# One recurrence kernel: the first inverse is served first, and other early work queues behind it

## The chip, the cores and the metric

The kernel runs on one core of a Trainium2 chip. The metric is the device time of one execution in microseconds (us); of several runs the median is taken. The engines are PE (matrix multiply), DVE (vector), ACT (scalar), POOL (GpSimd) and SP (whose queue issues most transfers). Each engine takes its own instructions strictly in order; semaphores make it wait for others.

## The reference

A linear-attention recurrence over 4 x 8 heads, 768 tokens and head size 40, followed by a mixture of experts. Cut to what matters:

```
for t in range(768):                       # per batch and head
    y[t] = r[t] @ state
    Sa = state @ a[t]
    state = state * w[t] - outer(Sa, b[t]) + outer(v[t], k[t])
x = y as [3072, 320]
P = exp(x @ w_gate - max), then 8 rounds of row and column normalisation
out = sum over 8 experts of P[:, e] * (relu(x @ w1[e]) @ w2[e])
```

## The kernel before

The 768 tokens are cut into 12 chunks of 64. Heads go in pairs, four pairs to a batch element, so the work comes in 12 x 4 = 48 units (chunk c, batch element b), numbered 0 to 47 in the order of need (unit 4c + b). Three kinds of work make up the first 500 us:

- **A preparation** (`prep`, one per unit, also numbered 0 to 47). It loads the unit's input (`inp`, 451.5 KB, SP queue), forms running products of the decay on DVE (`q` L124, its reciprocal L128, `g` L134), scales keys and `a` by them (`kb` L147, `ab` L153 and L154: on DVE for the first six preparations except that most `kb` are on POOL, later all on POOL), multiplies them on PE (`ll` L159, and the transposes `kt` L167), and puts the results into one of 20 operand sets (`sx` by DVE L169 and ACT; `bb`, `cc`). It sends `lt`, a part of the product, to DRAM (`ld`). POOL clears each set's `bb` once (L102).
- **An inverse** for each group of two chunks (`GROUPS`; 8 preparations, 128 small triangular matrices at once, one per partition). `load_lu` reads `ld` back into `lu` (L380), the steps of `INV` run on DVE (lines 184 to 207, nearly all through the scratch tile `pr`), `finish` (L369) flips the last part and writes the result to DRAM (`ud`, `nd`). `tload` reads it back in another layout for a chunk (`td`, `tt`, `lg`) and `tmat` completes it on PE and ACT (`gp` L261, `op` L266). An inverse needs the `ld` of all eight preparations of its group; a unit of chunks 0 and 1 needs inverse 0, of chunks 2 and 3 inverse 1, and so on up to inverse 5.
- **The recurrence** (`recur`, five steps for each unit): `av` on PE, `f` on DVE (L290), `xc` on PE, copies `x` and `c` on ACT, then `pu` on PE (L308), the first that needs the inverse, `pm` on DVE (L310), `c` on PE (L315), `ws` on DVE, `y` and `z` on POOL, and `zt` back to the next chunk's `vz`. I call the one `pu` of unit n "pu n"; it is 8 matmul records in the trace, 4 calls in the program.

Preparation n uses set n modulo 20, so preparations run up to 20 units ahead. From 500 us on, the experts run with PE nearly always busy.

The order on each engine is fixed when the kernel is built. `attention` makes a list `ev` of (time, function) with rule-of-thumb times, calls the functions in that order, and a scheduler then sorts each engine's instructions by that priority, the dependences, the free buffers and its own timing model. The first eight preparations have times from -20 on, the clears of `clear` come at `T_CLEAR`, the later preparations at -8 and above, and a step of chunk c at 5c and above; still, an instruction that could run early in the scheduler's model is placed early. Input tiles are borrowed from operand sets that are not yet in use (`IN_SETS`, `IN_SEQ`), as are the early `kb` and `lt` (`KB_SETS`).

## Time and profile before

| | |
|---|---|
| median of 3 runs | 1837.43 us (1831.14 to 1840.81) |
| profiled execution, its own time | 1831.31 us |
| its span in the trace | 1829.5 us |
| PE busy | 1729.6 us, 95% of the span |
| DVE / ACT / POOL busy | 1370.8 / 855.2 / 877.5 us |

"Busy" sums instructions of an engine; "granted clock" (PEclk) is the share of full TensorE speed in a stretch, so at 0.50 the same matmul lasts about twice as long and still counts as busy. Rows of the timeline give start, duration, engine, line, output<-input and a count. A row with SPq or ACTq is the issue of a transfer. Line numbers in rows of the profile are those of the kernel before.

### The profile page before, as it was taken

Reading aid. Unit: us, or ns where it says so; the run is one execution under the profiler, and the core shown is the slowest. Engines: PE = TensorE matmul, PEld = TensorE weight load, DVE = VectorE, ACT = ScalarE, POOL = GpSimd, SP = SyncE. Lnnn points to the kernel's source line nnn. Section 1 sums busy time; section 2 is a strip of 40 time slices with the busy share of each in tenths; the row PEclk is TensorE's granted clock in tenths of the full one; section 3 lists DMA queues with packets and bytes.
Section 4 is the critical chain, followed back from the end, with each engine's and each line's share of the span. In section 5 each row is a group of like instructions: output and inputs, shape, how many; then the busy total and the mean of one; then the engine's idle time right before and its main releaser. Section 6 shows DMA issues by size and latency. Waiting matters only on the chain.

```text
span 1829.5 us, 31656 instructions
## 1 busy us (share of the span) xinstructions
PE 1729.6 (95%) x11843; PEld 1701.8 (93%) x11843; DVE 1370.8 (75%) x2356; ACT 855.2 (47%) x1848; POOL 877.5 (48%) x851
## 2 busy tenths in 40 slices
PE   5479999999889999999999999999999999999999
PEld 4478889889879999999999999999999999999999
DVE  7876977974798867777686878977686877767676
ACT  6347767756643533434343434345343343424342
POOL 6545655721662626547191735007182644628160
PEclk8569999989899999999999999999999999999999
DMA  7467878766620101111020112201020111102001
GB/s 193 128 150 173 191 181 178 183 139 135 176 77 20 57 20 57 38 39 57 20 75 20 57 37 61 69 1 60 16 76 20 57 38 38 57 20 75 13 26 44
DMA packets 211759, 140.47 MB, mean 77 GB/s; under 512 B 162965, under 2 KB 193813, under 8 KB 211605
## 3 DMA queue, kind: packets, MB, share of 16 engines
q1 hardware_dynamic: 207925, 132.70, 27.9%
q10 hardware_dynamic: 3680, 5.74, 1.2%
q8 instruction: 94, 1.54, 0.4%
q14 instruction: 60, 0.49, 0.1%
HBM read 110.78 MB, written 27.61 MB: 76 GB/s over the span
## 4 chain that ended last, share of the span: by engine, by line
PE 77%; DVE 6%; DMA 4%; issue 4%; POOL 2%; SPq 2%; ACT 2%; ACTq 0%; POOLq 0%; DVEq 0%
PE op L647 36%; PE p L582 33%; PE xc L297 2%; DMA inp<-in_inp_dram 1%; PE ll L159 1%; PE pu L308 1%; PE c L315 1%; PE av L289 1%; DMA xs<-xd 1%; DVE g L134 1%; POOL ab L153 1%; PE op L266 1%; DVE hl L606 1%; DVE pr L193 1%; DVE q L124 1%
## 5 line engine op out<-in xcount | busy, mean ns | idle before, releaser
L582 PE MATMUL p<-xch,wh 128*128 128x384 f32 (+1 forms) x1792 | 605.3, 339 | 9.3 <-DVE sm L600 5.6
L603 ACT ACTIVATE hh<-sm 128x384 fp32r<-128x384 f32 x512 | 269.4, 526 | 725.4 <-DVE sm L600 725.4
L647 PE MATMUL op<-wh,hh 128*128 128x320 f32 x1536 | 476.5, 311 | 1.4 <-ACT hh L603 1.3
L647 PE MATMUL op<-wl,hh 128*128 128x320 f32 x1536 | 474.3, 309 | 0.0
L647 PE MATMUL op<-wh,hl 128*128 128x320 f32 x1536 | 466.7, 309 | 0.7 <-DVE hl L606 0.7
L528 POOL TENSOR_TENSOR wl<-ws,wh 128x640 fp32r<-128x640 f32 x60 | 103.1, 1718 | 606.1 <-ACT wh L526 605.8
L606 DVE SCALAR_TENSOR_TENSOR hl<-sm,hh 128x384 fp32r<-128x384 f32 x512 | 373.0, 762 | 2.3 <-ACT hh L603 2.0
L582 PEld LDWEIGHTS p<-xch,wh 128*128 128x128 f32 (+1 forms) x1792 | 337.4, 188 | 13.1 <-DVE sm L600 6.8
L582 PE MATMUL p<-xcl,wh 128*128 128x384 f32 x896 | 302.6, 338 | 0.0
L582 PE MATMUL p<-xch,wl 128*128 128x384 f32 x896 | 301.7, 337 | 0.0
L647 PEld LDWEIGHTS op<-wh,hh 128*128 128x128 f32 x1536 | 289.9, 189 | 2.2 <-ACT hh L603 2.2
L647 PEld LDWEIGHTS op<-wl,hh 128*128 128x128 f32 x1536 | 290.7, 189 | 0.0
L647 PEld LDWEIGHTS op<-wh,hl 128*128 128x128 f32 x1536 | 286.4, 188 | 1.1 <-DVE hl L606 0.9
L600 DVE TENSOR_TENSOR sm<-p,u 128x384 f32<-128x384 f32 x384 | 234.4, 620 | 8.8
L582 PEld LDWEIGHTS p<-xcl,wh 128*128 128x128 f32 x896 | 168.8, 188 | 0.0
L582 PEld LDWEIGHTS p<-xch,wl 128*128 128x128 f32 x896 | 168.6, 188 | 0.0
L600 DVE TENSOR_TENSOR sm<-p,p 128x384 f32<-128x384 f32 x128 | 71.3, 557 | 129.0 <-PE p L582 72.4
L600 DVE TENSOR_TENSOR p<-p,p 128x384 f32<-128x384 f32 x128 | 71.1, 556 | 101.2 <-PE p L582 100.6
L600 DVE TENSOR_TENSOR u<-p,p 128x384 f32<-128x384 f32 x128 | 70.7, 553 | 58.0 <-PE p L582 56.7
L536 POOL TENSOR_TENSOR wl<-ss,wh 128x512 fp32r<-128x512 f32 x60 | 89.8, 1497 | 30.8 <-ACT wh L533 26.7
L321 POOL TENSOR_TENSOR y<-ws,gl 104x256 f32<-104x256 f32 x48 | 43.1, 897 | 121.5 <-DVE ws L317 88.7
L159 PE MATMUL ll<-ab,kb 104*128 104x128 f32 x336 | 63.0, 345 | 37.2 <-POOL kb L147 16.7
(163 smaller groups left out, 2758.0 us busy)
## 6 DMA issues: line engine op xcount, KB each, us to landing
ws<-in_wts_dram SPq DMA_DIRECT2D x60, 832.0 KB, 4.5
inp<-in_inp_dram SPq DMA_DIRECT2D x42, 451.5 KB, 4.4
gd<-g SPq DMA_DIRECT2D x48, 113.8 KB, 2.8
gl<-gd SPq DMA_DIRECT2D x48, 113.8 KB, 2.9
vz<-in_v_dram SPq DMA_DIRECT2D x48, 112.0 KB, 3.3
xd<-y SPq DMA_DIRECT2D x24, 224.0 KB, 3.5
ld<-lt ACTq DMA_DIRECT2D x40, 128.0 KB, 2.7
rb<-in_r_dram SPq DMA_DIRECT2D x96, 48.0 KB, 2.9
```

The costliest lines, as they stand in the source:

```text
L124: nc.vector.tensor_tensor_scan(out=qr.rearrange("r p t -> r (p t)"), data0=w65[:, 260:0:-1], data1=one65, initial=0.0, op0=ALU.mult, op1=A ...
L134: nc.vector.tensor_tensor_scan(out=ge.rearrange("r p t -> r (p t)"), data0=w65[:, 0:260], data1=g1.rearrange("r p t -> r (p t)"), initial= ...
L159: nc.tensor.matmul(ll[:, p], lhsT=kb[:, p], rhs=ab[:, p], start=True, stop=True)
L297: nc.tensor.matmul(xc[h][:, p], lhsT=pp["sx"][:, p, h], rhs=f[:, p, h], start=True, stop=True)
L321: nc.gpsimd.tensor_tensor(out=y[0:R2, :, b % 2], in0=ws[:, :, 0:64], in1=gl[0:R2, :, 0:64], op=ALU.mult)
L528: g.tensor_tensor(out=wl[:, 0:640], in0=raw[:, 256:896], in1=wh[:, 0:640], op=ALU.subtract)
L536: g.tensor_tensor(out=lv[:, 3:7], in0=so[:, :, 0], in1=hv[:, 3:7, 0], op=ALU.subtract)
L582: nc.tensor.matmul(o, lhsT=w_, rhs=x_, start=(j == 0), stop=(j == 3))
L600: eng.tensor_tensor(out=out, in0=x, in1=y, op=ALU.add)
L603: nc.scalar.activation(out=hh[:, f, h], in_=sm[f][:, h], func=AF.Relu)
L606: v.scalar_tensor_tensor(out=hl[:, f, h], in0=sm[f][:, h], scalar=0.0, in1=hh[:, f, h], op0=ALU.max, op1=ALU.subtract)
L647: nc.tensor.matmul(ops[i], lhsT=a[:, h, cs], rhs=w_[:, cw], start=(f == 0 and h == 0 and j == 0), stop=(last and h == 1 and j == 2))
```

## The change

Nine inputs instead of six are borrowed or taken at the start (`IN_SETS` and `IN_SEQ` name more sets), and `g1`, `q`, `kb` and `lt` get two buffers instead of one. The first eight `ld` stores are issued by ACT instead of SP. Half of the second chunk's `load_lu`, the `nd` stores of inverse 0 and the four `tt` loads of chunk 0 go from SP to ACT as well, and chunk 0's `tload` is called inside `finish`. The memsets of `clear` are split: those that the first preparations need come at the very start, the rest (`lg`, `c1`, `tt`, `y`) go to POOL behind a mark. `mark` remembers one instruction of an engine, and `behind(...)` adds, for every instruction made inside it, an ordering edge to the mark of its own engine. The marks are: on ACT and SP the last `load_lu` transfers of inverse 0 (on ACT, for the clears, the last of the eight stores), on DVE the last copy of inverse 0, on POOL the last `ab` of preparation 7. Behind the marks go the steps of chunk 0 and preparations 9 to 19. Preparation 8 is left free. The scratch area reserved for software-made transfers is set to 1024 bytes; the kernel issues its transfers from SP and ACT.

```diff
-    g1_b = [pin.tile([RL, NP, 65], F32, name=f"g1{i}") for i in range(1)]
+    g1_b = [pin.tile([RL, NP, 65], F32, name=f"g1{i}") for i in range(2)]
...
+    for t in vz_b + rb_b:
+        nc.vector.memset(t, 0.0)
+    for t in (unf, tnf):
+        nc.gpsimd.memset(t, 0.0)
+    nc.gpsimd.memset(unf[:, 0:1024:33], 1.0)
+
     def clear():
-        nc.gpsimd.memset(unf, 0.0)
-        nc.gpsimd.memset(unf[:, 0:1024:33], 1.0)
-        nc.gpsimd.memset(tnf, 0.0)
-        for t in vz_b + rb_b + c1_b + lg_b:
-            nc.vector.memset(t, 0.0)
-        for t in y_b:
-            nc.gpsimd.memset(t[96:RL], 0.0)
-        for t in tt_b:
-            nc.gpsimd.memset(t, 0.0)
+        with behind(mybir.EngineType.Pool):
+            for t in lg_b + c1_b + tt_b:
+                nc.gpsimd.memset(t, 0.0)
+            for t in y_b:
+                nc.gpsimd.memset(t[96:RL], 0.0)
+
+    marks = {}
+
+    def mark(ins):
+        marks[ins.ins.engine] = ins.ins
+        return ins
+
+    def behind(*engines):
+        stack = ExitStack()
+        for e in engines:
+            stack.enter_context(tc.issue_after(marks[e]))
+        return stack
...
+    def send_l(c, b, lt, ld):
+        s, cc = GRP[c]
+        m = nc.scalar.dma_start(out=ld[cc, :, b], in_=lt)
+        if c * NB + b == N_FIRST - 1:
+            mark(m)
...
-        qr = pin.tile([RL, NP, 65], F32, name="q")
+        qr = pin.tile([RL, NP, 65], F32, name="q", bufs=2)
...
-            kb = pin.tile([R2, NP, 2, 64], F32, name="kb")
-            lt = pin.tile([64, NP, 2, 64], F32, name="lt")
+            kb = pin.tile([R2, NP, 2, 64], F32, name="kb", bufs=2)
+            lt = pin.tile([64, NP, 2, 64], F32, name="lt", bufs=2)
...
-        eng.tensor_tensor(out=ab[64:104, :, 64:128], in0=a_in[64:104], in1=g[64:104], op=ALU.mult)
+        m = eng.tensor_tensor(out=ab[64:104, :, 64:128], in0=a_in[64:104], in1=g[64:104], op=ALU.mult)
+        if cb == N_FIRST - 1:
+            mark(m)
...
-                nc.sync.dma_start(out=tt[r, :, r], in_=ud[u[blk][h]].rearrange("g j s -> j g s"))
+                (nc.sync if c else nc.scalar).dma_start(
+                    out=tt[r, :, r], in_=ud[u[blk][h]].rearrange("g j s -> j g s"))
...
-        nc.vector.tensor_copy(out=tn[us, 16:32, 0:16], in_=un[us, 0:16, 16:32].rearrange("u c j -> u j c"))
+        last = nc.vector.tensor_copy(out=tn[us, 16:32, 0:16], in_=un[us, 0:16, 16:32].rearrange("u c j -> u j c"))
         for o in range(0, us.stop, 64):
             nc.sync.dma_start(out=invs[s][1][o:o + 64], in_=un[o:o + 64])
-            nc.sync.dma_start(out=invs[s][2][o:o + 64], in_=tn[o:o + 64])
+            (nc.sync if s else nc.scalar).dma_start(out=invs[s][2][o:o + 64], in_=tn[o:o + 64])
+            if s == 0 and o == 0:
+                mark(last)
+                tload(0)
...
-                    nc.sync.dma_start(
+                    m = (nc.scalar if s == 0 and cc and h else nc.sync).dma_start(
...
+                    if s == 0 and cc and not h:
+                        mark(m)
...
-        next(gens[c, b], None)
+        with behind(*(() if c else marks)):
+            next(gens[c, b], None)
...
-        preps[c, b] = prep(c, b, invs[s][0])
+        with behind(*(marks if N_FIRST < c * NB + b < NSX else ())):
+            preps[c, b] = prep(c, b, invs[s][0])
...
-IN_SETS = (16, 15, 14, 13)
+IN_SETS = (16, 15, 14, 13, 18, 17, 19)
-IN_SEQ = (16,15,14,13,0,0,16,15)
+IN_SEQ = (16, 15, 14, 13, 18, 17, 0, 0, 19, 16, 15, 18, 17)
-N_SP = 8
+N_FIRST = 8
-T_CLEAR = -19.95
+T_CLEAR = -19.925
```

What this does to the order shows at three places. In the rows below the numbers behind names (`ab_203`) tell buffers apart; lines are those of each kernel's own file, and the changed file is 21 to 24 lines longer there (L124 becomes L145, L159 L182, L167 L190, L169 L192, L308 L332, L310 L334).

On DVE, the first steps of inverse 0. Before (`st` as the output is `sx` of a preparation):

```order
L200 COPY lu<-lu 128x2x8x8
L201 COPY lu<-lu 128x16x16
L184 TENSOR_TENSOR pr<-un,lu 128x4
L134 SCALAR_TENSOR_TENSOR g<-inp,g_205 112x260
L187 TENSOR_REDUCE un<-pr 128x4
L184 TENSOR_TENSOR pr<-un,lu 128x16
L187 TENSOR_REDUCE un<-pr 128x4x2
L169 TENSOR_TENSOR st_158<-ll,cst 64x8x64
L184 TENSOR_TENSOR pr<-un,lu 128x36
```

The same place now, from the last two `sx` of the first eight preparations on:

```order
L192 TENSOR_TENSOR sx_187<-ll,cst 64x8x64
L192 TENSOR_TENSOR sx_190<-ll,cst 64x8x64
L223 COPY lu<-lu 128x2x8x8
L224 COPY lu<-lu 128x16x16
L207 TENSOR_TENSOR pr<-un,lu 128x4
L210 TENSOR_REDUCE un<-pr 128x4
L207 TENSOR_TENSOR pr<-un,lu 128x16
L210 TENSOR_REDUCE un<-pr 128x4x2
```

Between the first and the last row of inverse 0, DVE had 26 instructions of other preparations; now it has one, the `sx` of preparation 8.

On DVE, where inverse 1 begins. Before, between the last copy of inverse 0 (L369) and the start of inverse 1 (L200) stand the four instructions of one preparation:

```order
L369 COPY tn<-un 128x16x16
L124 SCALAR_TENSOR_TENSOR q<-inp,cst 112x260
L128 RECIPROCAL g_205<-q 112x4
L134 SCALAR_TENSOR_TENSOR g<-inp,g_205 112x260
L169 TENSOR_TENSOR st_165<-ll,cst 64x8x64
L200 COPY lu<-lu 128x2x8x8
L201 COPY lu<-lu 128x16x16
```

Now 53 instructions stand there (11 `q`, 11 reciprocals, 11 `g`, 8 `sx`, 5 `f`, 3 `ws`, 4 `pm`); the last of them and the start of inverse 1:

```order
L341 TENSOR_TENSOR ws<-c_1332,c_206 104x416
L334 TENSOR_TENSOR pm<-pu,cst 128x416
L145 SCALAR_TENSOR_TENSOR q<-inp,cst 112x260
L149 RECIPROCAL g_200<-q 112x4
L155 SCALAR_TENSOR_TENSOR g<-inp,g_200 112x260
L223 COPY lu<-lu 128x2x8x8
L224 COPY lu<-lu 128x16x16
```

So inverse 1 went from before the first `pm` to behind the fourth. From its first row to its last copy DVE now has the 39 instructions of the inverse, 2 copies of inverse 2's input, 10 `sx`, 9 `q`, 8 reciprocals, 7 `g`, 5 `f`, 5 `ws`, 4 `pm` and 2 small copies `lg`; inverse 2 begins in the row after it.

On PE, the rows ahead of the first `pu`. Before:

```order
L159 MATMUL ll<-ab_204,kb 128x128 x4
L167 MATMUL kt<-cst,kb 128x104 x4
L261 MATMUL gp<-td,lg 64x32 x8
L266 MATMUL op<-td,lg 64x32 x8
L261 MATMUL gp<-td,lg 64x32 x8
L308 MATMUL pu<-x_948,tt_199 128x104 x4
```

Now:

```order
L285 MATMUL gp<-td,lg 64x32 x8
L182 MATMUL ll<-ab_197,kb 128x128 x4
L190 MATMUL kt<-cst,kb 128x104 x4
L290 MATMUL op<-td,lg 64x32 x8
L285 MATMUL gp<-td,lg 64x32 x6
L182 MATMUL ll<-ab_198,kb 128x128 x4
L190 MATMUL kt<-cst,kb 128x104 x4
L285 MATMUL gp<-td,lg 64x32 x2
L332 MATMUL pu<-x_939,tt_193 128x104 x4
```

Preparations now stand between the steps that complete the inverse, but there are fewer of them ahead of the first `pu`. Counted over the PE order, and over the DVE order for the inverses:

| ahead of pu number | 1st | 4th | 8th | 9th | 14th | 24th | 48th |
|---|---|---|---|---|---|---|---|
| preparations begun, before | 18 | 20 | 24 | 24 | 31 | 40 | 48 |
| preparations begun, now | 12 | 17 | 24 | 29 | 32 | 41 | 48 |
| matmul calls, before | 184 | 284 | 452 | 490 | 708 | 1124 | 1996 |
| matmul calls, now | 136 | 260 | 444 | 528 | 720 | 1128 | 2002 |

| last copy of inverse | 0 | 1 | 2 | 3 | 4 | 5 |
|---|---|---|---|---|---|---|
| stands behind pm number, before | none | 4 | 13 | 22 | 30 | 36 |
| now | none | 8 | 12 | 20 | 28 | 37 |

Inverse 1 is needed from the 9th `pu` on, inverse 2 from the 17th, inverse 3 from the 25th, inverse 4 from the 33rd, inverse 5 from the 41st.

More of the change, by code (lines that the diff above doesn't have):

```diff
@@ L161, in prep @@
             nc.scalar.activation(out=lt, in_=ll[64:128], func=AF.Copy, scale=-1.0)
-            (nc.sync if cb < N_SP else nc.scalar).dma_start(out=ld[GRP[c][1], :, b], in_=lt)
+            send_l(c, b, lt, ld)
             kt = pt.tile([128, NP, 2, 64], F32, name="kt", tag="pt")
@@ L177, in prep @@
         if cb >= NKB:
-            (nc.sync if cb < N_SP else nc.scalar).dma_start(out=ld[GRP[c][1], :, b], in_=lt)
+            send_l(c, b, lt, ld)
         return dict(cc=cc, g=gd, sx=sx, bb=bb)
@@ L400, in attention @@
         t = 5 * c + 2 - T_LEAD
-        ev.append((t - L_LEAD, tload, (c,)))
+        if c:
+            ev.append((t - L_LEAD, tload, (c,)))
         for half in range(2):
@@ L823 @@
     from concourse.bass_utils import run_bass_kernel_spmd as _run
-    nc = _bacc.Bacc("TRN2", target_bir_lowering=False, num_devices=1)
+    nc = _bacc.Bacc("TRN2", target_bir_lowering=False, num_devices=1, dynamic_dma_scratch_size=1024)
     lay = _layout(inputs)
```

## The prediction

> **What bounds the kernel now.** I read the top of the page first, then a table of stretches, then the timeline around the inverses, and the DVE and POOL groups of the early stretches.
>
> ```profile
> span 1829.5 us, 31656 instructions
> PE 1729.6 (95%) x11843; PEld 1701.8 (93%) x11843; DVE 1370.8 (75%) x2356; ACT 855.2 (47%) x1848; POOL 877.5 (48%) x851
> 4.00:8.00 4.00, 0.00 (x0) 0.00 (x0) 3.64 (x7) 3.63 (x11) 3.88 (x5) 1.00 1.01 295
> 56.00:76.00 20.00, 8.82 (x39) 7.54 (x38) 18.54 (x41) 7.13 (x19) 11.22 (x13) 0.50 0.43 126
> 76.00:96.00 20.00, 8.32 (x36) 7.35 (x36) 19.14 (x23) 7.93 (x21) 13.14 (x13) 0.50 0.46 120
> 136.00:156.00 20.00, 19.80 (x206) 18.80 (x205) 17.49 (x29) 16.35 (x42) 17.07 (x20) 1.00 0.83 199
> 172.00:227.00 55.00, 49.73 (x463) 47.16 (x462) 51.34 (x90) 38.89 (x98) 35.18 (x41) 0.94 0.84 188
> 600.00:1829.00 1229.00, 1223.75 (x7691) 1222.59 (x7689) 907.57 (x1542) 495.20 (x976) 568.78 (x490) 1.00 0.13 43
> ```
>
> The stretches give, after their length, the busy time of PE, weight loads, DVE, ACT and POOL, then the granted clock, the DMA share and GB/s. From 600 us on PE is busy 1223.75 of 1229 us: nothing there can move, and a gain or loss of the first 500 us arrives whole at the end. From 56 to 96 us, inverse 0, DVE is full (37.7 of 40) and PE is half empty at half clock. From 136 us on PE is nearly full; from 172 to 227, inverse 2, DVE is again the fuller (51.3 of 55 against 49.7). So three things can be bought: an earlier first `pu`, fewer stretches in which an inverse fills DVE, and less waiting for an inverse.
>
> **The change, part by part.** The stations of the run before:
>
> ```profile
> 7.37 0.63 DVE L124 TENSOR_TENSOR_SCAN q<-st,cst 112x260 f32<-112x260 f32 x1
> 23.55 0.70 DVE L124 TENSOR_TENSOR_SCAN q<-st,cst 112x260 f32<-112x260 f32 x1
> 37.71 0.66 DVE L124 TENSOR_TENSOR_SCAN q<-st,cst 112x260 f32<-112x260 f32 x1
> 46.61 0.68 DVE L169 TENSOR_TENSOR sx<-ll,cst 64x512 f32<-64x512 f32 x1 [0.49 <-PE ll L159]
> 56.32 0.27 DVE L200 COPY lu<-lu 128x128 f32<-128x128 f32 x1 [0.61 <-DMA ld<-lt]
> 97.53 0.57 DVE L369 COPY tn<-un 128x256 f32<-128x256 f32 x1
> 113.67 2.03 PE L308 MATMUL pu<-x,tt 128*128 128x104 f32 x8
> 148.34 0.37 DVE L369 COPY tn<-un 128x256 f32<-128x256 f32 x1
> 177.38 1.14 PE L308 MATMUL pu<-x,tt 128*128 128x104 f32 x8
> 226.00 1.04 PE L308 MATMUL pu<-x,tt 128*128 128x104 f32 x8
> 308.71 1.84 PE L308 MATMUL pu<-x,tt 128*128 128x104 f32 x8
> 377.56 1.06 PE L308 MATMUL pu<-x,tt 128*128 128x104 f32 x8
> 393.35 1.43 PE L308 MATMUL pu<-x,tt 128*128 128x104 f32 x8
> ```
>
> The `q` rows are preparations 0, 3 and 7, the `sx` is preparation 7's; inverse 0 runs from 56.32 to 98.1, inverse 1 ends at 148.7; the `pu` rows are the 1st, 9th, 14th, 24th, 32nd and 33rd.
>
> Step 1, inverse 0 starts earlier. From preparation 0 to 3 the pace was 16.2 / 3 = 5.4 us each, from 3 to 7 14.2 / 4 = 3.5, because the first three share DVE, POOL and SP with the clears and with chunk 0's first `av`, `f` and `xc`. These now stand behind inverse 0, so all eight go at 3.5: the last `q` at 7.4 + 7 x 3.54 = 32.2 instead of 37.7. From the last `q` to the inverse it was 18.6 us. On POOL, clears of later sets stood ahead of the last `kb`, on SP inputs and `gd` of later preparations ahead of the stores; without these I take 14, so the inverse starts at 46. Bounds: 11 us from the last `q` (43), or all 18.6 (51). The nine inputs are 4.06 MB; at the 295 GB/s of 4 to 8 us they take 14 us and are in by 18, ahead of their use at 32, so this early load costs nothing; the cover goes if the preparations run faster than 2 us each.
>
> Step 2, inverse 0 alone on DVE. Its 34 instructions through `pr`, and the means of the others that DVE runs there:
>
> ```profile
> 105.00:149.00 44.00, 24.02 (x34) 0.78 0.72 148
> L124 DVE TENSOR_TENSOR_SCAN q<-inp,cst 112x260 f32<-112x260 f32 x5 | 3.9, 783 | 1.4 <-DMA inp<-in_inp_dram 1.4
> L134 DVE TENSOR_TENSOR_SCAN g<-inp,g 112x260 f32<-112x260 f32 x4 | 2.8, 688 | 0.0
> L290 DVE TENSOR_TENSOR f<-av,cst 104x512 f32<-104x512 f32 x4 | 2.7, 669 | 1.4 <-PE av L289 1.4
> L169 DVE TENSOR_TENSOR sx<-ll,cst 64x512 f32<-64x512 f32 x4 | 2.7, 667 | 0.0
> L317 DVE TENSOR_TENSOR ws<-c,c 104x416 f32<-104x416 f32 x4 | 2.3, 571 | 0.0
> L310 DVE TENSOR_TENSOR pm<-pu,cst 128x416 f32<-128x416 f32 x4 | 2.3, 563 | 0.0
> L128 DVE RECIPROCAL g<-q 112x4 f32<-112x4 f32 x5 | 0.8, 165 | 0.0
> ```
>
> 24.0, five copies of at most 0.37 and one `sx` (0.67) are 26.4 us, where it took 41.8. Preparation 8's `sx` is late on POOL (it stands behind some 6 us of clears), but POOL starts on these while the stores land, so I cost that wait at nothing, at most 3 us. Inverse 0 ends at 46 + 26.4 = 72.4, 25.7 us earlier than at 98.1.
>
> Step 3, to the first `pu`: it was 15.6 us. Two `nd` stores and four `tt` loads leave SP, but preparations 9 to 11 now begin only at 72.4 and stand on PE ahead of this `pu`. POOL makes them:
>
> ```profile
> L147 POOL TENSOR_TENSOR kb<-inp,q 104x512 f32<-104x512 f32 x11 | 14.0, 1270 | 17.2 <-DVE q L124 11.3 <-PE kt L167 3.5 <-issue 1.1
> L154 POOL TENSOR_TENSOR ab<-inp,g 40x256 f32<-40x256 f32 x10 | 9.1, 914 | 0.8
> L153 POOL TENSOR_TENSOR ab<-inp,g 40x256 f32<-40x256 f32 x10 | 8.9, 888 | 8.7 <-issue 6.6 <-DVE g L134 2.2
> L152 POOL COPY st<-q 104x4 f32<-104x4 f32 x8 | 4.0, 498 | 7.2 <-DVE q L124 7.1
> L102 POOL MEMSET st<- 128x416 f32 x6 | 2.5, 443 | 0.7 <-DMA ld<-st 0.6
> ```
>
> That is 3.6 us for each preparation, 4.0 with the clear: 12 us for three, then their `ll` and `kt`. So I leave 15.6: the first `pu` at 88.0 (85 to 92), a lead of 25.7.
>
> Two pages bear on this step. The transfers first: four `tt` issues on SP took 2.08 us.
>
> ```profile
> 105.35 2.08 SPq L252 DMA_DIRECT2D tt<-ud  x4
> 106.00:116.00 10.00, 7.55 (x60) 7.19 (x60) 7.86 (x23) 3.77 (x10) 1.39 (x2) 0.50 0.96 191
> 126.00:136.00 10.00, 10.00 (x89) 9.55 (x89) 8.64 (x12) 5.82 (x14) 5.87 (x5) 0.91 0.45 111
> ```
>
> The Trainium skill ("Trainium Kernel Development and Optimization", Key Constraints) says that SP and ACT issue to the same 16 DMA engines, so that a second issuing engine saves only issue time; the DMA share of 0.96 above agrees that the engines themselves are taken. By it the moved issues save at most those 2.08 us here, and the sum would end at 1824 instead of 1826.
>
> The clock second: PE idles through inverse 0, so the work behind it starts at half clock, as from 56 to 96 us. From 106 to 116 PE was busy 7.55 of 10 us and still had 0.50; 0.91 came with 126 to 136. The Trainium skill ("TensorE: Matmul & The Clock Gate", Part 1) gives full rate after one busy window of about 3.4 us, which would save some 4 us of PE work ahead of the first `pu` and end at 1822 at best; the stretch above does not bear it out, so half clock until well behind the first `pu` is in my sum.
>
> Step 4, inverse 1 is pushed back. It used to run from 106 to 148.7 beside chunk 0. Now 53 DVE instructions lie between inverse 0 and 1: 11 `q` 8.6, 11 reciprocals 1.8, 11 `g` 7.6, 8 `sx` 5.3, 5 `f` 3.3, 3 `ws` 1.7, 4 `pm` 2.3, together 30.6 us. But POOL has nine preparations (9 to 17) there, 9 x 3.57 = 32.1, six clears 2.7, and by estimate 5 for three pairs of `y` and `z` (1.6 a pair, less than a `kb` and an `ab`, since their tiles are smaller): 40 us. POOL is later than DVE, so inverse 1 starts at 72.4 + 0.7 + 40 = 113. Behind it DVE has 25.7 of the inverse, 0.6 of copies, 10 `sx` 6.7, 9 `q` 7.0, 8 reciprocals 1.3, 7 `g` 4.8, 5 `f` 3.3, 5 `ws` 2.9, 4 `pm` 2.3, `lg` 0.3: 54.9. In 105 to 149 such a sum was used up without a hole, so inverse 1 ends at 168 (DVE alone: 158; with as much waiting again as POOL adds: 178). The 9th `pu` comes 15.6 later, at 183.6, where it was 177.4. The lead of 25.7 is a lag of 6.2. Who waits: all of chunk 2, and PE, which from the 8th `pu` on has only preparations left.
>
> Step 5, what is bought with it. The five preparations that PE has more behind it at the 9th `pu` are work of the next stretch, and inverse 2, which began at 172.5 and filled DVE until 227, now follows inverse 1 at once. From the 9th to the 14th `pu` it took 48.6 us for 218 calls, 0.223 each; from the 14th to the 24th 82.7 us for 416 calls, 0.199, where PE sets the pace. Now there are 192 calls, and with inverse 2 largely done I take the pace of PE: 38.2 us, the 14th `pu` at 221.8 instead of 226.0, a lead of 4.2 us. One preparation is still ahead there: its `ll` and `kt` are 1.68 us.
>
> ```profile
> 181.29 1.16 PE L159 MATMUL ll<-ab,kb 104*128 104x128 f32 x8
> 190.74 0.52 PE L167 MATMUL kt<-cst,kb 104*128 104x104 f32 x4
> 171.53 5.03 DMA inp<-in_inp_dram
> ```
>
> Step 6, less waiting for inverses 3 and 4. They ended two units ahead of their use, now four. The 33rd `pu` came 15.8 us after the 32nd, where a unit takes 8.3; so up to 7.5 us were lost there. I take 5 (0 to 12, since inverse 3 may give some as well). The larger buffers and the smaller scratch area cost nothing by themselves.
>
> Sum: -4.2 - 1.7 - 5 = -10.9 us. The profiled execution took 1831.3 us (span 1829.5 and 1.8 around it), which gives 1820.4. It lies 6.1 below the median of the runs shown, 1837.4; against that median, 1826.
>
> **The rivals.**
>
> (a) Much better, 1814. POOL is not late: alone, `kb` and `ab` are shorter than these means, which come from a stretch where DVE was full. Then inverse 1 starts with the 30.6 of DVE, 9.4 us earlier, and two later waits go: -11 - 9.4 - 3 = -23. For it: the means are high against the shortest rows. Against it: DVE is just as full now.
>
> (b) No change, 1835 to 1838. Step 5 pays nothing, because PE is at 49.7 of 55 there anyway: then the lag of 6.2 stands against five preparations of 1.68 (8.4), -2 us, and step 6 may be another issue order and give nothing. The same comes out if the change does not do what it says: if the first eight preparations keep 5 us each, inverse 0 starts at 54, all is 8 us later, and -11 becomes -3.
>
> (c) Slower, 1846. SP is in order too. Behind the inverse it gets `load_lu` of inverse 1 ahead of the inputs of preparations 16 on, and the first four of those loads wait for the store of preparation 11. An input took 5.03 us on the chain (row above); if four of them (16 to 19) are fetched one after the other, 20 us are added to step 4, inverse 1 ends at 188 and the 9th `pu` at 204. -11 + 20 = +9. It decides once inverse 1 ends later than 188; the prefetch of six inputs ahead of the inverse speaks against it.
>
> **How the numbers follow.** My case gets 0.42, (a) 0.18, (b) 0.28, (c) 0.12. Half a per cent, 9.2 us, is about what a measurement of this kernel can tell from no change; that is 1828.2. Of my case (1818 to 1834 by the bounds of steps 1, 4 and 6) some two thirds lie below, 0.28, which with (a) makes 0.46 faster; 0.14 and (b) make 0.42 the same; (c) is 0.12 slower. The range is 1811 to 1843: it cuts (c) at its lower half and the far end of (a).
>
> **What would show it.** Right: the first `lu` copy near 46, the last copy of inverse 0 near 72, the first `pu` near 88, inverse 1 from about 113 to 168, the 9th `pu` near 184 and the 14th near 222; POOL full from 73 to 113. Wrong: a first `lu` copy behind 51 (step 1), a hole of several us in inverse 0 at preparation 8's `sx` (step 2), a DVE that waits for inputs between the inverses (rival c), or a 9th to 14th `pu` no closer than before (step 5).

## The result: slower, and inverse 1 is 21 us later than forecast

The changed kernel took 1854.53 us (median of 5 runs, 1849.85 to 1860.02), beside 1837.43 for the kernel before (5 runs, 1831.14 to 1841.80). The ratio is 1.0096, with a 95% interval of 1.0069 to 1.0124: 17 us slower, where 1826 was forecast. The profiled execution took 1851.92 us, so it stands 2.6 below its median, as that of before stood 6.1 below; spans of single profiles are therefore compared with some caution, and the verdicts below rest on medians.

The top of the page, and then the stretches that answer to those of the prediction (length; busy time of PE, weight loads, DVE, ACT, POOL; granted clock, DMA share, GB/s):

```profile
span 1850.1 us, 31613 instructions
PE 1734.0 (94%) x11843; PEld 1705.3 (92%) x11843; DVE 1360.1 (74%) x2354; ACT 855.6 (46%) x1848; POOL 869.3 (47%) x854
49.00:76.00 27.00, 4.31 (x20) 3.65 (x19) 25.56 (x40) 1.86 (x5) 1.27 (x3) 0.50 0.61 145
80.00:100.00 20.00, 18.80 (x114) 17.57 (x113) 10.02 (x17) 14.36 (x36) 14.71 (x24) 0.50 0.64 129
100.00:120.00 20.00, 19.86 (x181) 18.98 (x180) 8.66 (x15) 14.29 (x35) 10.05 (x15) 0.91 0.89 168
180.00:200.00 20.00, 6.12 (x28) 5.27 (x28) 15.03 (x29) 8.85 (x25) 10.11 (x12) 0.55 0.84 191
```

The engines do the same work as before (PE 1734.0 us against 1729.6), so the loss is mostly waiting. The first stretch is inverse 0: DVE is full, and PE, ACT and POOL together do 7.4 us of work in 27. Between 80 and 120 it is the other way round: PE has hardly a free us and DVE is busy 18.7 of 40. From 180 to 200 PE has 6.1 us of work in 20, because units from the 9th on wait for inverse 1.

The stations, as rows of the timeline (start, duration, engine, line, operation, in brackets the idle time ahead of it and what ended it):

```profile
49.30 0.27 DVE L223 COPY lu<-lu 128x128 f32<-128x128 f32 x1 [7.98 <-DMA lu<-ld]
75.90 0.37 DVE L393 COPY tn<-un 128x256 f32<-128x256 f32 x1
97.29 2.03 PE L332 MATMUL pu<-x,tt 128*128 128x104 f32 x8
134.09 0.27 DVE L223 COPY lu<-lu 128x128 f32<-128x128 f32 x1 [0.89 <-DMA rb<-in_r_dram]
191.99 0.35 DVE L393 COPY tn<-un 128x256 f32<-128x256 f32 x1
208.13 2.01 PE L332 MATMUL pu<-x,tt 128*128 128x104 f32 x8
250.30 0.39 PE L332 MATMUL pu<-x,tt 128*128 128x104 f32 x2
520.00 1.03 PE L332 MATMUL pu<-x,tt 128*128 128x104 f32 x8
```

Inverse 0 runs from 49.3 to 76.3 and ends 22 us earlier than before. But inverse 1 starts at 134.1 (before 106.3), ends at 192.3 (148.7), and the 9th `pu` comes at 208.1 (177.4), the 14th at 250.3 (226.0; the row has its first two records), the 48th at 520.0 (498.65). The lead of 22 us is a lag of 31 at the 9th `pu`, and 21 of it reach the end.

What DVE waited for from 76 to 135, and POOL and ACT from 50 to 135 (sum, times, longest):

```profile
DVE q L145 <- DMA inp<-in_inp_dram: 16.0, 5, 4.9
DVE q L145 <- POOL kb L168: 3.9, 2, 2.0
POOL kb L168 <- DVE q L145: 26.8, 1, 26.8
ACT st L178 <- DMA td<-ud: 29.1, 1, 29.1
```

POOL and ACT stand still for 27 and 29 us, the whole of inverse 0: nothing is left for them that is not queued behind it. (The text on the change names the last `load_lu` as ACT's mark for the preparations too; in the code only SP's `load_lu` is marked, and ACT's mark is the last of the eight stores. So it is through `q` on DVE, and through ACT's own `nd` and `tt` transfers, that the two stand still.) And the five `q` that wait for inputs, those of preparations 15 to 19, stand on DVE ahead of inverse 1, such as these two:

```profile
104.86 0.78 DVE L145 TENSOR_TENSOR_SCAN q<-inp,cst 112x260 f32<-112x260 f32 x1 [4.90 <-DMA inp<-in_inp_dram]
131.55 0.70 DVE L145 TENSOR_TENSOR_SCAN q<-inp,cst 112x260 f32<-112x260 f32 x1 [3.82 <-DMA inp<-in_inp_dram]
```

### The profile page after: what moved, and what is told of

Its sections match the earlier page's. It is cut to its first block, busy times and chain, and to the rows that moved or that the text cites. A ratio compares the mean times of both kernels' runs of the same rounds, so it can differ in the third digit from the quotient of the medians.

```text
span 1850.1 us, 31613 instructions
## 1 busy us (share of the span) xinstructions
PE 1734.0 (94%) x11843; PEld 1705.3 (92%) x11843; DVE 1360.1 (74%) x2354; ACT 855.6 (46%) x1848; POOL 869.3 (47%) x854
## 4 chain that ended last, share of the span: by engine, by line
PE 73%; DVE 4%; DMA 1%; issue 1%; ACT 1%; POOL 0%; SPq 0%; ACTq 0%; DVEq 0%; POOLq 0%
PE op L679 35%; PE p L614 32%; PE xc L321 1%; DVE hl L638 1%; PE pu L332 1%; PE av L313 1%; DVE sm L632 1%; PE c L339 1%; PE op L290 1%; PE gp L285 0%; PE lp L369 0%; PE zt L359 0%; DVE u L632 0%; DMA inp<-in_inp_dram 0%; DVE p L632 0%
## 5 line engine op out<-in xcount | busy, mean ns | idle before, releaser
L632 DVE TENSOR_TENSOR sm<-p,p 128x384 f32<-128x384 f32 x128 | 71.3, 557 | 130.3 <-PE p L614 72.7
L632 DVE TENSOR_TENSOR u<-p,p 128x384 f32<-128x384 f32 x128 | 70.8, 553 | 58.9 <-PE p L614 57.8
L743 DVE SCALAR_TENSOR_TENSOR acc<-op,pmat,acc 128x320 f32<-128x320 f32 x168 | 91.3, 544 | 4.5 <-PE op L679 4.4
## 6 DMA issues: line engine op xcount, KB each, us to landing
ld<-lt ACTq DMA_DIRECT2D x42, 128.0 KB, 3.0
```

The costliest lines, as they stand in the source:

```text
L632: eng.tensor_tensor(out=out, in0=x, in1=y, op=ALU.add)
L743: nc.vector.scalar_tensor_tensor(out=acc[:, m], in0=ops[i], scalar=pmat[:, n, e:e + 1], in1=acc[:, m], op0=ALU.mult, op1=ALU.add)
```

## The experiments

All are edits of the changed kernel. The stations of each, from its trace (us; the time between the end of inverse 0 and the start of inverse 1 stands in the fourth column), and its median:

| run | inverse 0 | inverse 1 starts | behind inverse 0 | 9th `pu` | 48th `pu` | median | ratio to before, 95% |
|---|---|---|---|---|---|---|---|
| before | 56.3 to 98.1 | 106.3 | 8.2 | 177.4 | 498.7 | 1837.4 | 1 |
| changed | 49.3 to 76.3 | 134.1 | 57.8 | 208.1 | 520.0 | 1854.5 | 1.0069 to 1.0124 |
| e1 four inputs | 45.8 to 73.3 | 125.7 | 52.4 | 201.4 | 512.7 | 1843.2 | 1.0012 to 1.0052 |
| e2 16 to 19 held on DVE | 47.9 to 74.8 | 124.9 | 50.0 | 201.8 | 518.5 | 1850.7 | 1.0040 to 1.0104 |
| e3 `gd` on ACT | 47.8 to 74.7 | 130.7 | 56.0 | 206.7 | 524.4 | 1855.7 | 1.0058 to 1.0108 |
| e4 9 to 19 free | 52.1 to 99.9 | 99.1 | -0.8 | 179.8 | 505.4 | 1833.4 | 0.9941 to 0.9983 |
| e5 9 to 13 free | 51.8 to 87.2 | 114.7 | 27.4 | 188.9 | 510.0 | 1846.3 | 1.0030 to 1.0070 |
| e6 e4 + four inputs | 53.1 to 106.6 | 105.8 | -0.8 | 184.5 | 507.5 | 1848.8 | 1.0030 to 1.0094 |
| e7 e1 + `kb` on DVE | 49.6 to 76.4 | 130.3 | 53.8 | 206.0 | 515.4 | 1851.7 | 1.0049 to 1.0113 |
| e8 e1 + PE busy, 16 | 47.3 to 74.9 | 128.1 | 53.2 | 201.8 | 515.6 | 1851.2 | 1.0056 to 1.0101 |
| e9 e1 + PE busy, 27 | 46.8 to 74.5 | 124.3 | 49.8 | 202.1 | 513.1 | 1846.3 | 1.0031 to 1.0066 |
| e10 e9 + `kb` on DVE | 47.7 to 75.3 | 126.4 | 51.1 | 201.7 | 506.8 | 1841.9 | 1.0007 to 1.0036 |
| e11 steps free | 54.8 to 81.6 | 138.4 | 56.8 | 209.6 | 531.7 | 1867.5 | 1.0145 to 1.0193 |
| e12 both free | 56.7 to 106.4 | 103.9 | -2.5 | 201.0 | 524.8 | 1847.0 | 1.0040 to 1.0083 |
| e13 e10 + less ACT | 48.1 to 75.0 | 123.2 | 48.2 | 207.8 | 511.0 | 1846.1 | 1.0022 to 1.0070 |
| e14 e1 + less ACT | 48.0 to 75.2 | 128.0 | 52.8 | 204.5 | 515.8 | 1847.9 | 1.0038 to 1.0079 |
| e15 9 to 15 free | 51.1 to 91.4 | 94.2 | 2.8 | 175.0 | 490.7 | 1832.8 | 0.9958 to 0.9999 |
| e16 e1 + less PE | 47.6 to 74.9 | 120.0 | 45.1 | 196.6 | 516.7 | 1853.4 | 1.0058 to 1.0127 |

(A negative figure: the first copy for inverse 1 stands ahead of the last one of inverse 0. The profiled executions of e15 and e6 lie 6 and 7 us below their medians, that of e12 12 us above its own, so its stations say little.) From the 48th `pu` to the end of the span all of these take 1328 to 1334 us: what is lost before stays lost.

### First question: the inputs, the SP queue, or the preparations themselves

e1 gives all inputs that are not borrowed from operand sets (those of preparations 6, 7 and 13 on, so the late ones, 15 to 19, among them) four buffers in place of two.

```diff
-... pin.tile([RL, 1032], F32, name="inp", bufs=2)
+... pin.tile([RL, 1032], F32, name="inp", bufs=4)
```

> The changed kernel with four reload buffers for inputs instead of two, nothing else. Measured of the changed kernel: DVE waits 16.0 us (5 times) for inputs between inverse 0 and inverse 1, inverse 1 starts at 134.1 us, the 9th pu at 208.1. Theory T1 (the two reload buffers make inputs 15 to 19 late, and their q stand ahead of inverse 1 on DVE): the waits fall to under 5 us, inverse 1 starts at 118 to 123, the 9th pu near 195, and the time falls by 10 to 14 us against the changed kernel, to about 1842. Rival T2 (SP's in-order queue makes the inputs late, whatever the buffers): waits stay over 10 us, time within 4 us of the changed kernel. Rival T3 (POOL and PE set this pace, the inputs only show it): waits fall, but DVE then waits as long for PE or POOL, inverse 1 stays behind 130, time within 4 us.

The input waits went, 11 of the 17 us came back, and inverse 1 started 8 us earlier; yet it still started 52 us behind inverse 0. Other waits took part of their place; the largest, from 76 to 126, is that for POOL's `kb` (7.0 us, where it was 3.9):

```profile
DVE q L145 <- POOL kb L168: 7.0, 6, 2.2
125.67 0.94 DVE L223 COPY lu<-lu 128x128 f32<-128x128 f32 x1 [1.69 <-DMA lu<-ld]
```

e2 holds the DVE instructions of preparations 16 to 19 behind the first copy of inverse 1, so that none of their `q` can stand ahead of it.

```diff
-        with behind(*(marks if N_FIRST < c * NB + b < NSX else ())):
+            st.enter_context(behind(*(marks if N_FIRST < cb < NSX else ())))
+            if 2 * N_FIRST <= cb < NSX:
+                st.enter_context(tc.issue_after(flips[1]))
```

> The changed kernel, with the DVE instructions of preparations 16 to 19 ordered behind the first copy of inverse 1, so that a late input of these four can hold up neither the sx of preparation 15 nor the inverse. T1: inverse 1 starts at 116 to 123 instead of 134.1 and the time falls by 8 to 14 us. T2: inputs 16 to 19 are as late, but they hold up nothing that inverse 1 needs, so the same gain; it does not tell T1 from T2. T3: inverse 1 starts behind 128 and the time is within 4 us, since preparations 9 to 15 are paced by POOL and PE.

Inverse 1 started 9 us earlier, took 57 us as in the changed kernel (58), and ended 10 us earlier; the 9th `pu` came 6.3 us earlier. But inverse 2, which needs preparations 16 to 23, started 11 us later (193.4 against 182.2), and the 14th `pu` came 3.1 us later (253.4):

```profile
181.62 0.38 DVE L395 COPY tn<-un 128x256 f32<-128x256 f32 x1
193.42 0.27 DVE L224 COPY lu<-lu 128x128 f32<-128x128 f32 x1 [3.77 <-DMA td<-ud]
```

The time came 4 us lower, 1850.7, too little to tell. What was won ahead of one inverse was lost ahead of the next.

e3 sends the `gd` stores of preparations 9 to 19 from ACT instead of SP.

```diff
-        nc.sync.dma_start(out=gd[:, 0:260], ...)
+        (nc.scalar if N_FIRST < cb < NSX else nc.sync).dma_start(out=gd[:, 0:260], ...)
```

> The changed kernel, with the gd stores of preparations 9 to 19 issued by ACT instead of SP (SP waited 20.9 us in 12 waits for g between 60 and 200 us). T2: SP reaches the inputs earlier, DVE's waits for inputs fall from 16.0 to under 8 us and the time by 5 to 10 us. T1: the inputs wait for their two buffers all the same, waits stay over 12 us, time within 4 us of the changed kernel. T3: within 4 us.

The time did not change (1855.7). Inverse 1 started 3.4 us earlier, and the waits for inputs ahead of it, here from 74 to 131, fell by half, from 16.0 us:

```profile
DVE q L145 <- DMA inp<-in_inp_dram: 8.8, 3, 4.6
```

So SP's order had a part in the waits, but not one that the time shows. Of the six input loads that SP issues from 98 to 130 us, five now follow within 0.9 us the `kb` on POOL that frees their buffer (in the changed kernel up to 3.6 us behind it): what lateness is left comes from the want of free buffers. The unchanged time agrees with the Trainium skill ("Trainium Kernel Development and Optimization", Key Constraints), which says that a second issuing queue saves issue time only.

e4 takes preparations 9 to 19 out from behind the marks; chunk 0's steps and the clears stay there.

```diff
-        with behind(*(marks if N_FIRST < c * NB + b < NSX else ())):
+        with behind(*(())):
```

> The changed kernel, with preparations 9 to 19 no longer ordered behind the marks; only chunk 0's steps and the clears are. Then preparations share DVE with inverse 0 again, inverse 0 ends near 95 us as in the kernel before, and inverse 1 ends behind the 4th pm. If the queueing of the preparations is what costs (T1, T2 and T3 all say so), the time comes back to the kernel before, 1832 to 1842. If something else of the change costs (stores on ACT, POOL's clears, buffers, chunk 0's steps held back), it stays over 1848.

1833.4: all 21 us came back, and the kernel is 0.4% faster than before (interval 0.17 to 0.59%). Inverse 0 takes 48 us instead of 27 here, but inverse 1 starts at its end:

```profile
99.09 0.23 DVE L223 COPY lu<-lu 128x128 f32<-128x128 f32 x1
99.53 0.35 DVE L393 COPY tn<-un 128x256 f32<-128x256 f32 x1
```

### Second question: which part, and which preparations

e11 frees chunk 0's steps and leaves the preparations behind the marks; e12 frees both, so that only the clears stay behind one.

```diff
-        with behind(*(() if c else marks)):
+        with behind():
```

> The changed kernel with chunk 0's steps not behind the marks; preparations 9 to 19 and the clears still are. If the preparations are the whole loss (as their release alone, 1833.4, says): within 4 us of the changed kernel, 1850 to 1858. If steps and preparations behind the inverse crowd each other, so that either one alone would do: 1836 to 1843.

> Neither chunk 0's steps nor preparations 9 to 19 behind the marks; only the clears are. What is left is the rest of the change: inputs loaded earlier, the first stores on ACT, half of the loads on ACT, two buffers of `q`, `kb`, `lt` and `g1`, clears split. If queueing chunk 0's steps is what made the run with free preparations a little faster than before (1833.4 against 1838.3): 1836 to 1840, no change. If the early loads and the ACT queue did: 1830 to 1835, a ratio of 0.995 to 0.998.

Both lie outside what was expected of them, and together with e4 they make a table that adds up (medians, us):

| | preparations 9 to 19 free | queued |
|---|---|---|
| chunk 0's steps free | 1847.0 (e12) | 1867.5 (e11) |
| chunk 0's steps queued | 1833.4 (e4) | 1854.5 (the change) |

Queueing the preparations costs 20.5 or 21.1 us, queueing the steps gains 13.6 or 13.0, whichever way the other is set. The four were timed in three sessions; by each one's ratio to the kernel before it is 20 or 25 and 13 or 18, so the sum holds to some 5 us. The rest of the change, e12 against before, costs 10. So the change holds one good part, chunk 0's steps behind inverse 0, with which inverse 0 starts some 5 us earlier. What in the rest costs the 10 us wasn't tried and stays open.

e5 and e15 free only some: 9 to 13 in the one, 9 to 15 in the other.

```diff
-        with behind(*(marks if N_FIRST < c * NB + b < NSX else ())):
+        with behind(*(marks if 15 < c * NB + b < NSX else ())):    # e15; 13 in e5
```

> The changed kernel, but preparations 9 to 13 may run beside inverse 0; only 14 to 19 queue behind its last copy. Theory A (cover: each preparation moved behind inverse 0 costs its share of the 21 us between the changed kernel and the one with all eleven free): five of eleven come back, about 10 us; inverse 0 ends near 87, inverse 1 starts near 118 and the time is 1841 to 1846. Rival B (the input reloads of preparations 15 to 19, still behind the inverse and still with two buffers, are the loss): inverse 1 still starts at 128 or later and the time stays at 1848 to 1854. Rival C (only the first five find free engines beside inverse 0, the other six fill DVE): all of it comes back, 1831 to 1836.

> The changed kernel, but preparations 9 to 15, those that inverse 1 needs, may run beside inverse 0; only 16 to 19 queue behind its last copy. With all eleven free it was 1833.4, with 9 to 13 free 1846.3. If each preparation behind the inverse costs its share: 1839 to 1843, inverse 1 starting near 105. If only those in front of inverse 1 cost: 1829 to 1834, inverse 0 ends near 92 and inverse 1 starts within 12 us of it.

With 9 to 13 free 8.2 us came back (1846.3), with 14 and 15 free as well another 13.5 (1832.8), and with 16 to 19 too nothing more (1833.4). A share for each preparation, which e5 alone would have allowed, is out: the whole loss lies with the seven preparations, 9 to 15, whose `ld` inverse 1 needs. The 13.5 us are not the work of 14 and 15 alone: in e5 the inputs of 16, 18 and 19 also kept DVE waiting for 8.3 us ahead of inverse 1, where e15 has only two `q` and one `f`. e15 shows what they do beside inverse 0:

```profile
51.00:91.00 40.00, 20.82 (x92) 18.55 (x92) 39.38 (x61) 18.20 (x45) 22.90 (x29) 0.59 0.48 114
91.02 0.37 DVE L393 COPY tn<-un 128x256 f32<-128x256 f32 x1
94.16 0.27 DVE L223 COPY lu<-lu 128x128 f32<-128x128 f32 x1 [0.98 <-DMA nd<-tn]
175.04 1.14 PE L332 MATMUL pu<-x,tt 128*128 128x104 f32 x8
```

They lengthen inverse 0 by 13 us (40 against 27), and in that time PE, ACT and POOL do 62 us of work instead of 7.4. Inverse 1 then starts 2.8 us behind inverse 0 instead of 57.8, and the 9th `pu` comes at 175.0, 33 us earlier than in the changed kernel. e4 and e15 are the two versions that beat both kernels; by 0.2 to 0.4%, less than the half per cent that one measurement can tell, though both intervals lie below 1.

e6 gives e4 the four input buffers.

```diff
-        with behind(*(marks if N_FIRST < c * NB + b < NSX else ())):
+        with behind(*(())):
...
-... name="inp", bufs=2)
+... name="inp", bufs=4)
```

> Preparations 9 to 19 free as in the run before (1833.4), and four input buffers in place of two. That run's DVE waited 9.1 us for inputs between 56 and 180 us. If inputs are late there as well and DVE, full through inverse 0, passes it on: 1826 to 1830. If the wait is on engines that something else holds up (PE nearly full from 110 us on): 1832 to 1836, with the waits gone or moved to POOL or PE.

A miss: 1848.8, 15 us slower than e4. The waits for inputs went as expected, but more preparations ran inside inverse 0 (10 `q` where e4 has 8), which ended at 106.6 instead of 99.9, and the first `pu` came at 127.2 instead of 115.1. That the two input buffers had held back work that is better held back is a reading of this and not shown: at the 48th `pu` the trace is only 2 us behind that of e4, and its execution lies 7 us below the median.

### Third question: what holds inverse 1 behind inverse 0

With the input waits gone, the seven preparations that inverse 1 needs, with the first DVE steps of the next ones, still took 52 us, in which DVE had 33.7 us of work and POOL 39.3. Each of the following takes a load off one engine, some by giving it to another.

e7 makes `kb` of preparations 9 to 19 on DVE.

```diff
-        (nc.gpsimd if cb in KB_POOL else eng).tensor_tensor(
+        (nc.vector if N_FIRST < cb < NSX else nc.gpsimd if cb in KB_POOL else eng).tensor_tensor(
             out=kb, ...
```

> The changed kernel with four input buffers (1843.2 with these alone), and `kb` of preparations 9 to 19 made by DVE in place of POOL: POOL loses 11 x 1.2 = 13 us, DVE gains about 11 x 0.75 = 8. With these four buffers DVE was busy 33.7 of 53 us between the inverses, POOL 39.3, PE 49.6 at a granted clock of 0.74. If POOL's pace sets the start of inverse 1 (step 4 of the prediction): it starts 6 to 9 us earlier, at 116 to 120, and the time is 1836 to 1840. If PE sets it: it starts within 2 us of 125.7 and the time is 1842 to 1846.

POOL was the pace of step 4 in the prediction. Relieved of 13 us, which cost DVE some 8, it brought no earlier start: inverse 1 came 4.6 us later than in e1 and the time was 8.5 us longer, outside both expectations. DVE was through at 123.5 and then waited for preparation 15's part of `lu`:

```profile
130.27 0.27 DVE L223 COPY lu<-lu 128x128 f32<-128x128 f32 x1 [6.75 <-DMA lu<-ld]
```

e8 and e9 keep PE busy beside inverse 0 with 16 and 27 multiplications whose result nobody reads.

```diff
+        if cb == N_FIRST:
+            with tc.issue_after(m.ins):                 # m: last transpose of preparation 8
+                for n in range(9):                      # e9; in e8 4 x 4
+                    wm = ps.tile([128, 512], F32, name="wm", tag="ps")
+                    for _ in range(3):
+                        nc.tensor.matmul(wm, lhsT=ident, rhs=cst[:, 148:660], start=True, stop=True)
```

> The changed kernel with four input buffers (1843.2), and 16 matrix multiplications of 128 x 512 whose result nobody reads, on PE behind the transposes of preparation 8, so in the time in which PE has nothing to do beside inverse 0. They add work and no result. At the granted clock of 0.50 each should last about 2.3 us, so PE is busy from about 50 to 76-87. If the half clock behind inverse 0 (0.50 until 100 us, PE full from 80 on) sets the pace there: the clock is 0.8 or more from 76 on, inverse 1 starts at 112 to 120 instead of 125.7 and the time is 1834 to 1839. If POOL or the chain between the engines sets it: the clock rises, inverse 1 starts within 2 us of 125.7, and the time is 1842 to 1845. If the dummies are still running when inverse 0 ends: the first `pu` comes later than 94 and the time is above 1845.

> The changed kernel with four input buffers (1843.2 with these alone), and 27 matrix multiplications of 128 x 512 whose result nobody reads, on PE behind the transposes of preparation 8. With 16 of them PE had the clock at 1.00 from 55 to 67 us, but then idled 9 us and was back at 0.50 when inverse 0 ended. At 0.87 us each 27 end at about 76, with inverse 0. If the half clock behind inverse 0 sets the pace there (PE busy some 22 us at 0.50 from 76 to 100, so 11 us of work at 1.00): the clock stays near 1.00 behind 76, inverse 1 starts at 113 to 119 instead of 125.7, the 9th `pu` comes at 189 to 195 instead of 201.4 and the time is 1831 to 1837. If POOL or the store and reload behind preparation 15 sets the pace: clock up, inverse 1 at 123 to 128, time 1841 to 1850.

In e8 they took about 1 us each instead of the 2.3 expected and ended at 67, PE then idled 9 us, and inverse 0 ended at half clock again, so e8 told nothing of the clock. In e9 the clock was 1.00 from 55 to 84:

```profile
51.00:53.00 2.00, 2.00 (x3) 0.73 (x3) 1.83 (x6) 1.53 (x4) 0.00 (x0) 0.50 1.05 268
53.00:55.00 2.00, 2.00 (x5) 0.83 (x4) 1.93 (x4) 0.00 (x0) 0.00 (x0) 0.77 1.01 264
67.00:76.00 9.00, 9.00 (x26) 4.20 (x25) 8.59 (x10) 0.00 (x0) 0.64 (x1) 1.00 0.09 20
76.00:84.00 8.00, 5.67 (x58) 5.04 (x56) 5.92 (x10) 2.52 (x7) 7.42 (x13) 1.00 1.06 209
84.00:88.00 4.00, 2.18 (x13) 1.86 (x12) 3.35 (x5) 3.89 (x10) 3.17 (x5) 0.58 0.40 89
88.00:92.00 4.00, 3.70 (x34) 3.64 (x35) 0.82 (x3) 3.74 (x11) 3.79 (x6) 0.50 0.55 121
```

At full clock PE had gaps (5.67 of 8 us busy), among them three of 0.8 us, for DVE's `f`, POOL's `ab` and the read-back of inverse 0. Then the clock fell again. Between the inverses it was 0.86 on average instead of 0.74 in e1, and inverse 1 moved by 1.3 us (2.6 counted from the end of inverse 0), where 7 to 13 were expected if the half clock set the pace. So the half clock of the first 8 us isn't the pace; a full clock all the way was not reached.

e10 has e9's busy PE and e7's `kb` on DVE together.

> As the run before, and `kb` of preparations 9 to 19 on DVE. So inputs, POOL and the PE clock are all relieved at once. If the three hold inverse 1 in turn: its start comes to 108 to 116 and the time to 1828 to 1836. If what is left is the chain through preparation 15 (its `ld` store, then `load_lu`, for which DVE waited 15.1 us with `kb` on DVE alone): it starts at 122 or later, with the same wait, and the time is 1843 to 1852.

The start stayed (126.4), with 4.9 us of waiting for `lu`; the time is 1841.9, 10 us better than e7 (half of it from a start 3.9 us earlier, half after the 9th `pu`) but no better than e1 by more than can be told. In 100 to 125 the trace shows PE without a gap (25.00 of 25 at clock 1.00) and ACT nearly so, with 23.21:

```profile
100.00:125.00 25.00, 25.00 (x254) 23.95 (x252) 20.45 (x34) 23.21 (x59) 15.06 (x23) 1.00 0.92 204
```

e13 (on e10, to POOL) and e14 (on e1, to DVE) take two of ACT's copies away.

```diff
-        nc.scalar.copy(out=sx[64:104, :, 0, 0:64], in_=ab[0:40, :, 0:64])
-        nc.scalar.copy(out=sx[64:104, :, 1, 0:64], in_=ab[64:104, :, 64:128])
+        cp = nc.gpsimd.tensor_copy if N_FIRST < cb < NSX else nc.scalar.copy   # e14: nc.vector
+        cp(out=sx[64:104, :, 0, 0:64], in_=ab[0:40, :, 0:64])
+        cp(out=sx[64:104, :, 1, 0:64], in_=ab[64:104, :, 64:128])
```

> As the run with four input buffers, the busy PE and `kb` on DVE (inverse 1 from 126.4, 1841.9), and the two copies of `ab` into `sx` of preparations 9 to 19 on POOL in place of ACT: ACT loses 2 x 0.40 us a preparation, 5.6 us up to preparation 15, POOL gains what `kb` took off it. ACT ran without a gap from 100 to 125 us there. If ACT is the last pace: inverse 1 starts at 118 to 122, and the time is 1834 to 1839. If it is the length of the chain within a preparation, whatever the engine: it starts at 125 to 129, and the time is 1840 to 1846.

> The changed kernel with four input buffers (inverse 1 from 125.7, 1843.2), and the two copies of `ab` into `sx` of preparations 9 to 19 on DVE in place of ACT. DVE was busy 33.7 of 53 us between the inverses and gets some 5 us more there. If ACT alone sets the pace: inverse 1 starts at 119 to 122 and the time is 1836 to 1840. If PE, POOL and ACT hold it at nearly the same time: within 2.5 us of 125.7, 1841 to 1846.

ACT's load fell (in 100 to 120 from 17.3 to 14.3 us in e14), and inverse 1 came 3.2 us earlier in e13 and 2.3 later in e14; both were slower than their bases. ACT isn't the pace either. What all these runs share is PE, in the stretch from 100 to 120 of e1, e13 and e14 in this order:

```profile
100.00:120.00 20.00, 20.00 (x195) 19.01 (x195) 14.15 (x24) 17.33 (x43) 16.05 (x22) 0.98 0.91 210
100.00:120.00 20.00, 20.00 (x207) 19.27 (x207) 17.15 (x31) 15.14 (x38) 18.22 (x26) 1.00 0.95 232
100.00:120.00 20.00, 20.00 (x206) 19.22 (x205) 19.45 (x31) 14.31 (x36) 14.30 (x19) 1.00 0.83 200
```

e16 therefore leaves out PE work: the `kt` transposes of preparations 9 to 15 (the copies read `ll` in their place).

```diff
+        elif N_FIRST < cb < 16:
+            kt = ll
...
-        for p in range(NP):
+        for p in range(0 if N_FIRST < cb < 16 else NP):
             nc.tensor.transpose(kt[:, p]...
```

> The changed kernel with four input buffers (inverse 1 from 125.7, 1843.2), without the `kt` transposes of preparations 9 to 15; the three copies that read `kt` read `ll` there, so ACT does as much as before. Left out: 28 calls on PE, at 0.9 us for four at half clock and 0.52 at full about 5 us. If PE's amount of work sets the start of inverse 1: it comes 4 to 6 us earlier, 119.5 to 122, and the time is 1837 to 1840. If no one engine sets it, but the row of seven preparations, each waiting for the one before on every engine: 123.5 to 127 and 1841 to 1845.

```profile
100.00:120.00 20.00, 18.91 (x181) 17.56 (x180) 13.88 (x24) 16.82 (x43) 16.58 (x23) 0.99 0.98 222
120.04 1.09 DVE L225 COPY lu<-lu 128x128 f32<-128x128 f32 x1 [0.19 <-DMA lu<-ld]
196.60 2.01 PE L334 MATMUL pu<-x,tt 128*128 128x104 f32 x8
```

This is the one relief that moved the start as its theory said, by 5.6 us for about 5 us of PE work (119.5 to 122 expected), and the 9th `pu` came 4.8 us earlier. The time didn't follow: 1853.4. The lead of 4.8 us was gone by the 24th `pu` (322.9 against 322.0 in e1) and a lag of 4.0 at the 48th. So for the start of inverse 1 PE's amount of work is the best supported pace, with one run for it; that this start alone sets the time isn't shown by e16. The leaving out also frees a PSUM tile for each preparation, of the two that `ll` and `kt` share, so the 5.6 us may not be PE's time alone.

## Why the prediction was wrong

**Step 1, right within its bounds.** Inverse 0 started at 49.3 (46 forecast, 43 to 51).

**Step 2, right.** Inverse 0 alone took 27.0 us (26.4), without a hole. It ended 21.8 us earlier than before (25.7).

**Step 3, 5.4 us short.** The first `pu` came 21.0 us behind inverse 0, not 15.6, so the lead was 16.4 instead of 25.7. I had left 15.6 although preparations 9 to 11 now stand among the steps that complete the inverse. PE was busy 18.8 us of the 20 from 80 to 100, at half clock. With the clock held up to 84 us (e9) the distance was still 19.5.

**Step 4 failed.** "POOL is later than DVE, so inverse 1 starts at ... 113": it started at 134.1, and the step's lag of 6.2 at the 9th `pu` became 30.8. This is 24.5 of the 32.3 us between the sum (-10.9) and the 48th `pu` (+21.4). The DVE work was counted rightly: behind its start inverse 1 took 58.3 us (54.9 forecast). What was wrong is the wait ahead of it, 57.8 us behind inverse 0 where I had 40.6; the other 3.9 us come from inverse 0, which ended at 76.3 and not at 72.4. I took the largest of two sums, DVE 30.6 and POOL 40, as if the other engines were free. Of the 17.2 us, 5.4 (57.8 against 52.4 in e1) are the inputs of preparations 15 to 19, reloaded through two buffers, the doubt of rival (c) with another cause than the SP queue. For the other 11.8 no single pace was shown: with POOL or ACT relieved, alone or together, inverse 1 still started at 123 to 130. PE, which had no term in step 4, is full there (busy 49.3 of the 52.4 us in e1): the preparations, the completion of inverse 0 and the first units of chunk 0 all reach it at once, after 27 us in which it had 4.3 us of work. Less work on it gave the earliest start with all eleven preparations queued, 120.0 (e16); beyond that one run it stays open whether PE is the pace.

The mistake behind it stands in the accounting. The prediction priced what inverse 0 loses to other work on DVE (41.8 against 26.4 us) and called its removal a gain. It did not price what the other engines did in that time: in e15, 62 us of PE, ACT and POOL work beside inverse 0, for 13 us of delay. e4, e5 and e15 show that this cover is worth the 21 us, and that all of it belongs to the seven preparations that the next inverse waits for.

**Step 5, right in sign.** The 9th to the 14th `pu` took 42.2 us (48.6 before): 6.4 gained of the 10.4 in the forecast of 38.2.

**Step 6, right in sign.** From the 14th to the 48th `pu` 269.7 us against 272.65 before, 3.0 gained where one preparation and the waits were to give 6.7. The 33rd `pu` now follows the 32nd by 6.8 us instead of 15.8, so the wait named there went; most of it came back elsewhere.

**The rivals.** (c) had the right sign and the right threshold: inverse 1 ended at 192.3, later than 188. Its mechanism, SP's order with `load_lu` ahead of the inputs, had a small part: these loads held SP from 100.8 to 103.7 us, and with the `gd` stores off SP the waits fell by half but the time did not change (e3). The larger cause is the two buffers (e1). (a) and (b) both needed a start of inverse 1 that no queued version reached.

**The clock.** The prediction doubted the rule of the Trainium skill ("TensorE: Matmul & The Clock Gate", Part 1) that a busy window of about 3.4 us gives full rate, since PE busy 7.55 of 10 us had stayed at 0.50. e9 agrees with the rule where matmuls follow without a gap: from 51 us on they reached 0.77 in 53 to 55 and 1.00 from 55. It changed no time: e9 is not faster than e1.

## What to carry to other kernels

Before an engine's rival work is moved behind a critical stretch, count what the other engines get done because of it in that stretch: removing 13 us of interference cost 21 us here, and the trace shows three engines that idled beside the stretch and had the same work to do later, all at once. Move out only what nobody waits for next (queueing preparations 16 to 19 cost nothing, 14 and 15 with them 13.5 us). And where several engines hand work on to each other, give each of them, PE too, its own sum before calling one the pace; taking one load away then mostly shows the next.

## What was not expected

The granted clock went from 0.50 to 1.00 within about 4 us of gap-free matmuls of 512 columns and stayed there for 8 us in which PE was busy 5.67, then fell at 84.6 us, although no gap on PE from 76 us to there was longer than 0.8 us (e9). In e1's 88 to 96 us, made of short matmuls and transposes, a PE that the profile shows as busy throughout stayed at 0.50:

```profile
88.00:92.00 4.00, 4.00 (x35) 3.68 (x34) 2.74 (x5) 3.51 (x10) 3.25 (x5) 0.50 0.61 139
92.00:96.00 4.00, 4.00 (x22) 3.68 (x22) 1.20 (x2) 2.21 (x7) 2.54 (x3) 0.50 0.18 49
```

And a small edit elsewhere moves what follows by several us: from the 9th to the 48th `pu`, where the code differs at most in the number of input buffers, the runs took between 303.2 us (e13) and 325.6 (e4), and the scheduler's new order of what follows is the likely reason. Effects of under some 8 us in the total, such as e10 against e1, are therefore not put down to a mechanism here (the 8 is a judgement from this spread), and the 10 us that e16 lost against e1 stay open. The 21 us do not hang on one pair: e4 against the change, e12 against e11 and e15 agree on them.
